# The router of three chunks six slots later in the MLP's schedule, the last chunk's router one slot later

## The chip, the cores and the metric

The kernel runs on one core of one Trainium2 chip. The metric is the device time of one launch in microseconds (us). The engines are called as the profile calls them: PE is TensorE with its matmuls, PEld its weight loads, DVE is VectorE, ACT is ScalarE, POOL is GpSimd, SP is SyncE, which here only issues DMAs.

## The reference

Three layers follow one another over 2304 tokens of width 512.

```python
# 1. attention, 4 batches x 8 heads x 576 positions x 64, causal window of 64
scores = scale * q @ k.T ; masked, softmax
x = attn @ v                                  # 2304 x 512
# 2. dense MLP
h = x @ w_in                                  # 512 -> 2048
g = h * (1.0 / (1.0 + np.exp(-1.702 * h)))
x = g @ w_out                                 # 2048 -> 512
# 3. mixture of 8 experts, two per token
logits = x @ w_gate
noise_scale = np.log1p(np.exp(x @ w_noise))
noisy_logits = logits + noise_scale * noise
top2 = two largest of the 8; their softmax gives the two weights
h = np.maximum(x[mask] @ w1[e], 0.0)          # 512 -> 1024, for the tokens that chose e
out[mask] += top2_w * (h @ w2[e])             # 1024 -> 512
```

## The kernel before, in words

Every operand of a matmul is split into two f16 parts, so one product is three matmuls (high by high, high by low, low by high).

The tokens are 18 tiles of 128, in six chunks of three tiles. Attention works tile by tile, the MLP chunk by chunk. While the MLP of chunk c runs, DVE, ACT and POOL also do the attention of later tiles and the routing of chunk c - 1.

**The slots.** From chunk 2 on the program is a list of slots. Each chunk has SL = 28 of them. Slots 0 to 15 are the first product, one block f of 128 of the 2048 hidden columns each (`s1mm`, line 665, 12 matmuls of 128x384). Slots 16 to 27 are the second product, four slots for each of three tiles (`s2_part`, line 700, 12 matmuls of 128x512 each). After the six chunks come the experts (lines 922 and 929), also slot by slot. Everything else is a task with a due time in slots, set by calls of `at(t, fn, ...)`. Tasks are sorted by due time, and before each slot those that are due are written into the program. So a due time fixes the place in the instruction streams of SP, POOL, DVE and ACT, each of which works strictly in that order. Only PE's order is not fixed so: the framework places PE's instructions by its own estimate of when their inputs are ready.

**The evacuation of a first-product block.** Block f's result lies in PSUM in one of two tiles named h or of two named y (blocks 2, 3, 6, 7, 10, 11 and 14 take y). ACT computes tanh of it into gf (`g_tanh`, line 670), DVE multiplies gf by the PSUM tile (`g_mul`, line 673, after which the PSUM tile is free), ACT writes the high part gb (line 676), POOL the low part (line 679). Block 13 needs the h tile of block 9, block 15 that of block 12.

**The attention beside it.** Per tile and group of heads: scores on PE (line 486) into s, mask and maximum on DVE (lines 552, 554), exponentials on ACT (line 560), normalisation on DVE (lines 564 to 570), a copy on ACT (line 578), its low part p on POOL (line 581), a transposing DMA from SP into PT (line 586), and the product with v on PE (line 621) into x, which ACT and DVE (lines 630, 636) copy into xT.

**The router of a chunk.** `x2t` issues a transposing DMA of the MLP's output R and stores R. `logits` (lines 748 to 751) is PE work on three tiles. Then nine blocks follow: `route_a` to `route_d` (softplus), `route_e` (lines 789 to 799: the noisy logits and the two largest), `route_f` (lines 804 to 817: one-hot masks, their sum r_M and the running count r_mc), `route_g` (lines 823 to 825: three small matmuls that count rows of each expert), `route_h` (lines 833 to 843: the weights), `route_i` (lines 850 to 865: the slots). Blocks e, f, h and i are about 40 small DVE instructions; f has one on ACT (line 804). Last, six `scatter` calls (line 877, indirect DMAs that POOL issues) write the rows' records into xmeta, from which the experts' gathers read.

With t0 = 28 (c + 1), the first slot of the next chunk, blocks e to i of chunk c stood at t0 + 10 to t0 + 14 and the scatters at t0 + 15 to t0 + 20, so in the next chunk's first product. For the last chunk (c = 5) the next chunk is the first expert. The router of chunk 0 is part of a hand-written list ahead of the slots.

Of the kernel before, what the change touches and what calls it, by code (L numbers as in the profile page):

```python
# [24 lines left out]
NCH = 6  # L25
# [10 lines left out]
P = dict(ld6=8, ld=8.93, q1=7, q2=5.75, v1=3.86, v2=3.85, pnorm=6, b3=0.0, b4=0.0, b5=-0.72, b6=0.01, b7=0.0,  # L36
         b8=0.94, l0=6.83, pv=8.27, tr=4.94, n1=3.81, x0=5.09, x1=1.5, r0=11.73, wo=5.88, wn=2.98, wc=1.03)
# [60 lines left out]
def fused_kernel(ctx, tc, q, k, v, w_in, w_out, w_gate, w_noise, noise, w1, w2, out, cap=CAP):  # L98
# [904 lines left out]
    def at(t, fn, *a):  # L1003
        tasks.append((t, len(tasks), fn, a))

    def base(i):
        c, j = divmod(i, 3)
        return SL * (c - 1) + 8 * j - 3

    for i in range(NPE, NTILE):  # L1010
        t0 = base(i)
# [20 lines left out]
    for c in range(NCH):  # L1032
        last = c == NCH - 1
        for j in range(3):
            d = 4 * j if c else 8 + 0.1 * j + P["r0"]
            l = (7 if last and j == 2 else 8) if c else P["l0"]
            at(SL * c + FS + d + (5 if c else P["x0"]), x2t, 3 * c + j)
            at(SL * c + FS + d + l, logits, 3 * c + j)
        t0 = SL * (c + 1)
        for fn, dt, dl in ((route_a, 5, 3.1), (route_b, 6, 3.2), (route_c, 7, 3.3), (route_d, 8, 3.4), (route_e, 10, 3.5),  # L1040
                           (route_f, 11, 3.6), (route_g, 13, 5), (route_h, 13, 5.2), (route_i, 14, 5.1)):
            if last and fn == route_i:
                dl = 5.3
            at(t0 + (dl if last else dt + (0 if c else P["l0"] - 8 + P["r0"])), fn, c)
        for j in range(3):
            for a in range(2):
                at(t0 + (5.4 if last else (15 if c else 17 + P["r0"]) + 2 * j + a), scatter, c, j, a)
    for n in range(4):
        at(2 * SL + 9 + 2 * n, zero_out, n)

# [18 lines left out]
    for e in range(1, E):  # L1069
        t0 = T6 + ES * (e - 1) + (10 if e == 2 else 0)  # L1070
# [3 lines left out]
    for e in range(E):  # L1074
        t0 = T6 + ES * (e - 1) if e > 1 else (t5 + 22 if e == 0 else T6 + P["x1"])
# [3 lines left out]
        t0 = T6 + ES * (e - 1) + 14 if e > 1 else T6 + 12 + e  # L1079
# [97 lines left out]
```

## Time and profile before

| | |
|---|---|
| median of 3 runs | 935.31 us (934.85 to 935.39) |
| the profiled execution | 933.35 us, its span 931.6 us |
| PE busy | 878.2 us, 94% of the span |
| PEld, DVE, ACT, POOL busy | 54%, 52%, 42%, 40% |
| mean granted clock of PE | 0.978 of full speed |

The span is the time from the first to the last instruction; the launch around it makes the rest of the profiled execution's time. Times in the views count from the span's start. A row of the timeline begins with its start and length; the brackets at its end hold the engine's idle time ahead of it and what ended that. Matmuls are pipelined, so the length of a row of matmuls is a little more than the distance to the next row's start; distances between starts are what adds up.

### The profile page before, as it was taken

Reading aid. Unit: us, or ns where it says so; the run is one execution under the profiler, and the core shown is the slowest. Engines: PE = TensorE matmul, PEld = TensorE weight load, DVE = VectorE, ACT = ScalarE, POOL = GpSimd, SP = SyncE. Lnnn points to the kernel's source line nnn. Section 1 sums busy time; section 2 is a strip of 40 time slices with the busy share of each in tenths; the row PEclk is TensorE's granted clock in tenths of the full one; section 3 lists DMA queues with packets and bytes.
Section 4 is the critical chain, followed back from the end, with each engine's and each line's share of the span. In section 5 each row is a group of like instructions: output and inputs, shape, how many; then the busy total and the mean of one; then the engine's idle time right before and its main releaser. Section 6 shows DMA issues by size and latency. Waiting matters only on the chain. (4 is left out here: it accounts for less than half of the span.)

```text
span 931.6 us, 16441 instructions
## 1 busy us (share of the span) xinstructions
PE 878.2 (94%) x6355; PEld 502.9 (54%) x6355; DVE 483.9 (52%) x1022; ACT 388.2 (42%) x884; POOL 372.0 (40%) x380
## 2 busy tenths in 40 slices
PE   5898998999899899999999999999999999999993
PEld 4664554545445545545544556674655656474651
DVE  8999976654825734742744522553443525252210
ACT  5888664636426524732633312351322315050200
POOL 2567674826625443551451621432313140323021
PEclk9889999999999999999999999999999999999997
DMA  9899999747887477521248674995866849392112
GB/s 249 215 229 197 232 214 186 129 80 184 238 148 136 81 137 137 81 60 46 91 128 202 142 148 80 231 262 120 192 149 132 209 99 242 48 259 36 23 25 36
DMA packets 255124, 135.90 MB, mean 146 GB/s; under 512 B 207456, under 2 KB 231680, under 8 KB 255040
## 3 DMA queue, kind: packets, MB, share of 16 engines
q1 hardware_dynamic: 218336, 74.28, 41.0%
q0 software_dynamic: 12160, 28.00, 14.3%
q10 hardware_dynamic: 24544, 32.51, 11.4%
q8 instruction: 52, 0.85, 0.4%
q14 instruction: 32, 0.26, 0.1%
HBM read 76.46 MB, written 21.07 MB: 105 GB/s over the span
## 5 line engine op out<-in xcount | busy, mean ns | idle before, releaser
L929 PE MATMUL o<-w,gb 128*128 128x512 f16 x960 | 210.1, 379 | 0.9 <-DVE gb L912 0.7
L700 PE MATMUL y<-w,gb 128*128 128x512 f16 x816 | 185.1, 380 | 0.0
L922 PEld LDWEIGHTS <-w 128*128 128x128 f16 x1536 | 150.1, 98 | 60.5
L952 POOL DMA_INDIRECT out_dram<-ot,me x40 | 69.5, 1739 | 234.7 <-DVE ot L949 228.0
L665 PEld LDWEIGHTS <-w 128*128 128x128 f16 x1152 | 111.5, 99 | 94.1 <-issue 23.1
L929 PEld LDWEIGHTS <-gb 128*128 128x128 f16 x960 | 93.4, 98 | 112.0 <-DVE gb L912 1.6
L665 PE MATMUL h<-xT,w 128*128 128x384 f16 x744 | 137.4, 338 | 14.7 <-DVE gf L673 12.1
L700 PEld LDWEIGHTS <-gb 128*128 128x128 f16 x864 | 82.3, 98 | 94.9 <-issue 1.2
L922 PE MATMUL h<-xe,w 128*128 128x384 f16 (+1 forms) x840 | 126.5, 302 | 0.0
L679 POOL TENSOR_TENSOR gb<-gf,gb 128x384 f16<-128x384 f32 x96 | 91.1, 954 | 81.5 <-ACT gb L676 81.3
L949 DVE TENSOR_SCALAR ot<-o,me 128x512 f32<-128x512 f32 x40 | 30.0, 751 | 144.3 <-PE o L929 122.1
L922 PE MATMUL y<-xe,w 128*128 128x256 f16 (+1 forms) x696 | 102.1, 297 | 0.0
L911 ACT ACTIVATE gb<-y 128x256 f16<-128x256 f32 (+1 forms) x58 | 24.9, 429 | 182.5 <-PE y L922 182.4
L265 DVE SCALAR_TENSOR_TENSOR w<-wst,w 128x1024 f16<-128x1024 f32 x64 | 78.5, 1227 | 40.2 <-ACT w L246 40.2
L246 ACT ACTIVATE w<-wst 128x1024 f16<-128x1024 f32 x64 | 67.5, 1056 | 30.6 <-DVE w L265 17.2
L906 POOL DMA_INDIRECT xg<-x2buf,me x40 | 42.8, 1069 | 72.3 <-DMA me<-xmeta 39.2
L665 PE MATMUL y<-xT,w 128*128 128x384 f16 x408 | 70.0, 326 | 1.5 <-DVE gf L673 1.5
L676 ACT ACTIVATE gb<-gf 128x384 f16<-128x384 f32 x96 | 49.2, 517 | 41.6 <-DVE gf L673 41.6
L560 ACT ACTIVATE sm<-sm,st 128x128 f32<-128x128 f32 x144 | 55.9, 391 | 11.0 <-DVE st L554 10.9
L911 ACT ACTIVATE gb<-h 128x384 f16<-128x384 f32 (+1 forms) x70 | 30.6, 438 | 68.1 <-PE h L922 67.2
L912 DVE SCALAR_TENSOR_TENSOR gb<-h,gb 128x384 f16<-128x384 f32 (+1 forms) x70 | 34.6, 494 | 41.6 <-ACT gb L911 41.6
L877 POOL DMA_INDIRECT xmeta<-rm,slot x36 | 38.5, 1070 | 39.9 <-DVE ov L865 31.5
(167 smaller groups left out, 936.7 us busy)
## 6 DMA issues: line engine op xcount, KB each, us to landing
wst<-in_moe_w_dram ACTq DMA_DIRECT2D x62, 512.0 KB, 4.1
wst<-in_moe_w_in_dram SPq DMA_DIRECT2D x16, 512.0 KB, 4.8
wst<-in_moe_w_out_dram SPq DMA_DIRECT2D x16, 512.0 KB, 4.3
vv<-in_v_dram SPq DMA_DIRECT2D x18, 256.0 KB, 4.8
x2buf<-R SPq DMA_DIRECT2D x18, 256.0 KB, 2.4
kq<-in_k_dram SPq DMA_DIRECT2D x16, 256.0 KB, 4.5
kq<-in_q_dram SPq DMA_DIRECT2D x16, 256.0 KB, 4.5
out_dram<-z POOLq DMA_DIRECT2D x3, 1280.0 KB, 6.2
```

Of the source, the lines that this page charges most:

```text
L246: act.activation(o[:, 0], i, AF.Copy, scale=s)
L265: dve.scalar_tensor_tensor(o[:, 1], i, s, o[:, 0], op0=ALU.mult, op1=ALU.subtract)
L560: act.activation(sm[:, u, :], sm[:, u, :], AF.Exp, bias=st[:, 0, u:u + 1], accum_out=st[:, 1, u:u + 1])
L665: pe.matmul(hp, w[:, a, d, fs], xt[:, x + d, :], start=n == 0, stop=n == 11)
L676: act.activation(g1[:, f, 0], GF[c, f], AF.Copy)
L679: pool.tensor_tensor(g1[:, f, 1], GF.pop((c, f)), g1[:, f, 0], op=ALU.subtract)
L700: pe.matmul(YP[i], g1[:, f, a, 128 * j:128 * j + 128], w[:, s, f % 8, :], start=f == 0 and a + s == 0, stop=f == 15 and a == 1)
L906: pool.indirect_dma_start(out=xg, out_offset=None, in_=src, in_offset=bass.IndirectOffsetOnAxis(ap=ME[e, part][:, t, 9:10], axis=0))
L911: act.activation(o[:, 0], hp, AF.Relu)
L922: pe.matmul(hp, w[:, a, d, 128 * f:128 * f + 128], x[:, s + d, :], start=m == 0, stop=m == 11)
L929: pe.matmul(yp, lhs[:, f, a, :], w[:, s, f, :], start=f == 0 and a + s == 0, stop=f == 7 and a == 1)
L952: s = pool.indirect_dma_start(out=out, out_offset=bass.IndirectOffsetOnAxis(ap=ids, axis=0), in_=ot, in_offset=None, compute_op=ALU.add)
```

## The change

For chunks 1, 2 and 3 the blocks e to i and the six scatters come six slots later, at t0 + 16 to t0 + 20 and t0 + 21 to t0 + 26, so in the second product. Blocks a to d stay. Chunk 4 is as it was. For the last chunk the logits of its third tile, all nine blocks and the scatters come one slot later.

```diff
-            l = (7 if last and j == 2 else 8) if c else P["l0"]
+            l = 8 if c else P["l0"]
...
-        for fn, dt, dl in ((route_a, 5, 3.1), (route_b, 6, 3.2), (route_c, 7, 3.3), (route_d, 8, 3.4), (route_e, 10, 3.5),
-                           (route_f, 11, 3.6), (route_g, 13, 5), (route_h, 13, 5.2), (route_i, 14, 5.1)):
-            if last and fn == route_i:
-                dl = 5.3
+        late = 0 if last or c == NCH - 2 else 6
+        for fn, dt, dl in ((route_a, 5, 4.1), (route_b, 6, 4.2), (route_c, 7, 4.3), (route_d, 8, 4.4),
+                           (route_e, 10 + late, 4.5), (route_f, 11 + late, 4.6), (route_g, 13 + late, 6),
+                           (route_h, 13 + late, 6.2), (route_i, 14 + late, 6.3)):
             at(t0 + (dl if last else dt + (0 if c else P["l0"] - 8 + P["r0"])), fn, c)
...
-                at(t0 + (5.4 if last else (15 if c else 17 + P["r0"]) + 2 * j + a), scatter, c, j, a)
+                at(t0 + (6.4 if last else (15 + late if c else 17 + P["r0"]) + 2 * j + a), scatter, c, j, a)
```

DVE near the end of chunk 2's first product, before the change: between the normalisation (line 570) and the product of block 12 (line 673) stands the whole of `route_h`.

```order
L570 TENSOR_TENSOR sm<-sm,st 128x512
L833 TENSOR_SCALAR r_wv<-r_wv 128x3
L834 TENSOR_SCALAR r_wv<-r_wv 128x3
L835 RECIPROCAL r_wv<-r_wv 128x3
L836 TENSOR_TENSOR r_wv<-r_wv 128x3
L838 TENSOR_TENSOR r_G<-r_oh_3412,r_wv 128x24
L839 TENSOR_TENSOR r_tg<-r_oh_3413,r_wv 128x24
L840 TENSOR_TENSOR r_G<-r_G,r_tg 128x24
L842 COPY rm<-r_G 128x3x8
L843 COPY rm<-idm 128x3x8
L673 SCALAR_TENSOR_TENSOR gf<-gf,h 128x384
L552 SCALAR_TENSOR_TENSOR sm<-s,msk 128x512
```

The same place now: the first four products are those of blocks 9, 10 and 11 (two in one row) and 12, then come 13 and 14.

```order
L673 SCALAR_TENSOR_TENSOR gf<-gf,h 128x384
L673 SCALAR_TENSOR_TENSOR gf<-gf,y 128x384 x2
L564 TENSOR_SCALAR st<-st 128x4
L565 RECIPROCAL st<-st 128x4
L570 TENSOR_TENSOR sm<-sm,st 128x512
L673 SCALAR_TENSOR_TENSOR gf<-gf,h 128x384
L552 SCALAR_TENSOR_TENSOR sm<-s,msk 128x512
L554 TENSOR_REDUCE st<-sm 128x4
L673 SCALAR_TENSOR_TENSOR gf<-gf,h 128x384
L673 SCALAR_TENSOR_TENSOR gf<-gf,y 128x384
L789 TENSOR_TENSOR r_ln<-r_ln,r_d 128x24
```

Blocks e, f and h of the router have left this stretch of DVE; block e (line 789) now begins behind the product of block 14.

On PE the three matmuls of `route_g` go with them. In chunk 2 they stood ahead of block 13 (first product, line 665). Now they stand in the second product (line 700), behind 36 of its matmuls, the scores of one group and one product with v; the rows around them are:

```order
 L700 LDWEIGHTS gb
 L700 MATMUL y<-w,gb 128x512
+L823 LDWEIGHTS u
+L823 MATMUL r<-r_M,u 128x24
+L824 LDWEIGHTS u
+L824 MATMUL r<-r_mc,u 128x24
+L825 LDWEIGHTS u
+L825 MATMUL r<-r_mc,u 128x8
 L700 LDWEIGHTS gb
 L700 MATMUL y<-w,gb 128x512
```

Chunks 3 and 4 change in the same way. In chunk 4, seven second-product matmuls that the framework had put ahead of block 15 now stand behind it.

On ACT, in the first expert (line 911 is the relu of an expert's first-product block, line 246 a weight cast), the router's two activations with their table loads come one relu later, and a weight cast stands between them:

```order
-L911 ACTIVATE gb<-h 128x384 x2
+L911 ACTIVATE gb<-h 128x384 x3
 L766 ACTIVATE r_t<-r_t 128x24
 L777 ACT_TABLE_LOAD
 L777 ACTIVATE r_ln<-r_u 128x24
+L200 DMA wst<-in_moe_w_dram 128x4x256
+L246 ACTIVATE w<-wst 128x4x256
 L804 ACT_TABLE_LOAD
 L804 ACTIVATE r_wv<-r_wv 128x3
-L911 ACTIVATE gb<-h 128x384
```

The relu of the fourth block thus runs ahead of the last chunk's router, on ACT and in the same way on DVE.

## Rows read from the trace of the kernel before

**Rows 1.** Stretches: from:to, length, PE, PEld, DVE, ACT, POOL busy, PEclk, DMA share, GB/s.
```profile
243.00:248.00 5.00, 2.92 (x12) 1.44 (x11) 4.59 (x20) 1.78 (x6) 1.47 (x2) 0.78 0.99 282
251.50:283.00 31.50, 31.50 (x260) 15.28 (x259) 10.71 (x20) 9.65 (x26) 13.26 (x11) 1.00 0.66 134
312.00:321.00 9.00, 6.13 (x67) 3.77 (x66) 7.50 (x26) 4.02 (x13) 4.15 (x4) 1.00 0.06 13
386.00:396.00 10.00, 7.83 (x89) 4.31 (x88) 8.45 (x33) 5.18 (x16) 4.22 (x5) 0.83 0.27 30
```

**Rows 2.** Timeline of PE, chunk 2, blocks 13 to 15 and after.
```profile
236.61 0.77 PE L486 MATMUL s<-kT,qT 128*128 128x64 f16 x24
238.27 0.17 PE L824 MATMUL r<-r_mc,u 128*128 128x24 f16 x1 [0.77 <-DVE r_mc L816]
...
245.24 3.47 PE L665 MATMUL h<-xT,w 128*128 128x384 f16 x12 [2.08 <-DVE gf L673]
...
251.46 0.77 PE L486 MATMUL s<-kT,qT 128*128 128x64 f16 x24
```

**Rows 3.** Timeline of PE, chunk 3, the same stretch.
```profile
311.95 0.77 PE L486 MATMUL s<-kT,qT 128*128 128x64 f16 x24
...
314.09 2.11 PE L665 MATMUL h<-xT,w 128*128 128x384 f16 x12
...
316.59 2.12 PE L665 MATMUL y<-xT,w 128*128 128x384 f16 x12
320.58 2.11 PE L665 MATMUL h<-xT,w 128*128 128x384 f16 x12 [1.86 <-DVE gf L673]
322.53 2.75 PE L700 MATMUL y<-w,gb 128*128 128x512 f16 x12
325.12 0.77 PE L486 MATMUL s<-kT,qT 128*128 128x64 f16 x24
325.82 2.76 PE L700 MATMUL y<-w,gb 128*128 128x512 f16 x12
```

**Rows 4.** Timeline of PE, chunk 4, the same stretch.
```profile
386.19 0.69 PE L486 MATMUL s<-kT,qT 128*64 128x64 f16 x32
389.05 1.98 PE L665 MATMUL h<-xT,w 128*128 128x384 f16 x6 [2.17 <-DVE gf L673]
...
398.13 2.11 PE L665 MATMUL h<-xT,w 128*128 128x384 f16 x12 [1.15 <-DVE gf L673]
...
401.25 0.69 PE L486 MATMUL s<-kT,qT 128*64 128x64 f16 x32
```

**Rows 5.** Timeline of all engines, chunk 2, around block 12's product.
```profile
241.06 0.47 ACT L670 ACTIVATE gf<-h 128x384 f32<-128x384 f32 x1
241.46 0.93 POOL L679 TENSOR_TENSOR gb<-gf,gb 128x384 f16<-128x384 f32 x1
241.53 0.89 DVE L833 TENSOR_SCALAR r_wv<-r_wv 128x3 f32<-128x3 f32 x1
...
244.64 0.55 DVE L673 SCALAR_TENSOR_TENSOR gf<-gf,h 128x384 f32<-128x384 f32 x1
```

**Rows 6.** Timeline of DVE, chunk 4, block e and the product behind it.
```profile
386.19 0.69 DVE L789 TENSOR_TENSOR r_ln<-r_ln,r_d 128x24 f32<-128x24 f32 x1
...
388.45 0.55 DVE L673 SCALAR_TENSOR_TENSOR gf<-gf,h 128x384 f32<-128x384 f32 x1
```

**Rows 7.** Timeline of SP, chunks 2 and 4: the transposes of p into PT.
```profile
233.64 1.83 SPq L586 DMA_TRANSPOSE PT<-p  x1
...
385.99 1.31 SPq L586 DMA_TRANSPOSE PT<-p  x1
```

**Rows 8.** Line 586 in chunk 4, from issue to landing.
```profile
DMA to landing us min/median/max: 4.2/4.2/4.2
```

**Rows 9.** Timeline of DVE, chunk 2's second product: the longest wait.
```profile
272.34 0.69 DVE L708 SCALAR_TENSOR_TENSOR R<-y,R 128x512 f16<-128x512 f32 x1 [8.61 <-ACT R L705]
```

**Rows 10.** Timeline of PE, first expert: the last chunk's counting matmul.
```profile
509.70 0.19 PE L823 MATMUL r<-r_M,u 128*128 128x24 f16 x1 [0.46 <-DVE r_M L812]
```

## The prediction, made before the changed kernel ran

> **What bounds the kernel now.** I read the page first: PE is busy for 94% of the span, so the kernel is as long as PE's work plus PE's waits, and other engines matter only where PE waits for them. Next the list of waits on PE, and then the timeline of PE chunk by chunk, to see where these waits lie. They repeat. In chunks 2, 3 and 4, at the end of the first product, PE stops twice within some 10 us: for r_M or r_mc of the router and for gf, the product that frees a PSUM tile [rows 2 to 4]. The second products have no such stop: PE is busy for 31.50 of 31.50 us in chunk 2's [rows 1].
>
> Then the reason, from the timeline of all engines. Block 15 of chunk 2 waited until 245.24 for the product of block 12, which DVE began at 244.64 [rows 2, 5]. Its input was ready long before: the tanh began at 241.06 and took 0.47, so 241.53. In between DVE worked through route_h, from 241.53 to 244.64, that is 3.11 us [rows 5]. The stall of 2.08 us is shorter than what stood in front of the product. In chunk 4 it is route_e that stands before block 9's product, from 386.19 to 388.45, and PE's block 13 begins at 389.05, when that product is done (388.45 + 0.55 = 389.00) [rows 4, 6]. So these stalls come from where the router's small instructions stand on DVE, not from a full DVE.
>
> The stalls cost more than their length. The granted clock is 0.78 of full speed from 243 to 248 us and 0.83 from 386 to 396, and 1.00 from 312 to 321 [rows 1]; block 15 took 3.47 us after the stall in chunk 2, and 2.11 after the shorter one in chunk 3 [rows 2, 3]. That is the lower of the two levels (1.2 instead of 2.4 GHz) for a few us behind idle times of 2.08 and 2.17 us.
>
> **The moved blocks e to i of chunks 1 to 3.** I take the stretch from the last scores ahead of block 13 to the next scores, and subtract what its work takes without stalls. Chunk 3 gives the parts as distances between starts [rows 3]: scores 325.82 - 325.12 = 0.70; block 13 with the product with v behind it 316.59 - 314.09 = 2.50; a block 322.53 - 320.58 = 1.95, needed twice (14 and 15); the first twelve of the second product 325.12 - 322.53 = 2.59. Sum 0.70 + 2.50 + 1.95 + 1.95 + 2.59 = 9.69. The stretches took
> - chunk 2: 251.46 - 236.61 = 14.85, so 5.16 lost [rows 2];
> - chunk 3: 325.12 - 311.95 = 13.17, so 3.48 lost [rows 3];
> - chunk 4: 401.25 - 386.19 = 15.06, so 5.37 lost [rows 4].
>
> Together 14.0 us, with the time at the lower clock in it. Now each stretch without the router in it.
>
> Chunk 2: DVE is some 3 us earlier at block 12 through route_h alone, and earlier again through e and f; block 15 could start at 236.61 + 0.70 + 2.50 + 1.95 = 241.8, and with h gone the product may start at 241.53 even if nothing before it moved. With e and f gone too I count no stall. What may come next is the product with v: PE gets to it at 236.61 + 0.70 + 1.95 = 239.3. Its PT was issued at 233.64; with a landing of 4.2 us (the nearest row with one, chunk 4) that is 237.8, in time [rows 7, 8]. At worst it landed when PE took it before, about 1.3 us later than PE now comes. I take 0, bounds 0 and 1.3.
>
> Chunk 3: nothing is late next by the same sum; the whole 3.48.
>
> Chunk 4: block 9's product can begin at 386.19, where route_e began, and end at 386.74; PE wants block 13 at 386.19 + 0.70 = 386.9. No stall. But the product with v behind it would be reached at 386.9 + 1.95 = 388.8, and its PT, issued at 385.99 with a landing of 4.2 us, comes at 390.2 [rows 7, 8]. That chain does not go through the router, so 1.4 us stay. They also give DVE the time to finish block 12. So 5.37 - 1.4 = 4.0, bounds 2.5 (another such wait at block 15, as the 1.15 us there now) and 5.4.
>
> What comes back: the three matmuls of route_g. 0.17 us is the length of one [rows 2], so three are 0.5 at most and, pipelined, nearer 0.1; for three chunks 0.3, bounds 0 and 1.5. The DVE work itself, about as many us as before, now lies beside a second product in which DVE is busy for 10.71 of 31.50 us, and has a wait of 8.61 us in one piece [rows 1, 9]; the six scatters lie on POOL, busy 13.26 there. This hides them. If the cover were gone, PE would wait at line 823, which stands in PE's queue behind 36 matmuls of the second product: chunk 2's would begin at 241.8 + 1.95 = 243.7, and line 823 is reached 3 x 2.59 + 0.70 + 0.55 = 9.0 later, at 252.7. r_M needs block 14's product (block 14 ends at 241.8, tanh and product 1.0), route_e (2.3 as in rows 6), block 15's product (0.55), the normalisation and block f; for the last two I allow 3.1, as much as block h took with all its delays [rows 5]. That is 248.8, so some 4 us of margin.
>
> One thing could eat into it. POOL's subtraction from 241.46 to 242.39 and DVE's line 833, a 128x3 instruction that took 0.89 and ended at 242.42, run side by side [rows 5]: DVE's instruction was held until POOL's was done. The Trainium skill, page "GPSIMD Engine Reference", section "Key points", says that GpSimd shares its SBUF interfaces with VectorE and that they contend where a DVE instruction runs in a two-port mode or has two SBUF inputs. Most of the router's small instructions have two, so by that rule they can be held in the second product as well; with one hold of 0.9 in each of e and f the sum would still be the same, since 1.8 is less than the margin. The hold that rows 5 show is in the price of the slower case below.
>
> **The last chunk, one slot later.** Its router costs PE 0.46 us before line 823 [rows 10]. Now the fourth relu goes ahead of it on ACT and DVE, so the router's chain starts about one block (1.95) later and has a weight cast in it, while line 823 stands behind 12 more first-product and 14 more second-product matmuls, 1.95 + 14 x 0.216 (2.59 / 12) = 5.0 us. The wait of 0.46 should go; in return the fifth and sixth relu stand behind block f, and PE's seventh block may wait for them a few tenths. I take 0, bounds -0.5 and +0.6. The scatters come some 3 us later; their rows are read much later, in the second part of the first expert.
>
> **Sum.** 5.2 + 3.5 + 4.0 - 0.3 + 0 = 12.4 us less. The profiled execution of 933.35 us (span 931.6 and 1.75 around it) would be 921.0. It lies 1.96 us below the median of the runs shown, 935.31, and I let that difference stand: 935.31 - 12.4 = 922.9.
>
> **Rivals.**
> 1. Attention keeps a part of the stalls. Normalisation and mask stay in front of block 12's product, and ACT's exponentials in front of its tanh. For it: in chunk 4 PE waits for gf twice, at blocks 13 and 15 [rows 4], so DVE is late there over a long stretch and not behind one block alone. Against it: the 3.11 us in front of a product that was ready. Then the waits for r_M and r_mc go (0.77 in chunk 2, 314.09 - 311.95 - 0.70 = 1.44 in chunk 3; 2.2) and a third of the rest of the 14.0 (11.8 / 3 = 3.9): 6.1 less, 929.2.
> 2. The stalls only change their place. PE gains at the first product and gives it back at line 823 or at the next product with v, us for us. For it: the 1.4 us in chunk 4 are of that kind. Against it: the margin of 4 us. Time 935.3.
> 3. Slower: the counting matmuls wait in PE's in-order queue. Block f stands behind the normalisation, and that behind ACT's exponentials. If that wait is as long as the longest one of DVE in this stretch, 8.6 [rows 9], and block f is held at every step as h was, 3.1 [rows 5], r_M is 11.7 late, 4 of it covered: 7.7 us in each of three chunks, 23.1 - 12.4 = 10.7 slower, 946.0. It decides from a lateness of 4 + 12.4 / 3 = 8.1 us. Against it: the 8.6 is a wait for the second product's own result late in the stretch, which the moved blocks come ahead of.
>
> **How the numbers follow.** My sum 0.68, rival 1 0.18, rival 2 0.06, rival 3 0.08. About 0.2% (1.9 us) is what a measurement of this kernel can tell from no change. Faster by more: 0.68 + 0.18 = 0.86; within 0.06; slower 0.08. The range goes at its low end to all 14.0 and the last chunk's 0.5 and a little (935.3 - 15.0 = 920.3), at its high end to rival 1 (929.2): 920.3 to 929.5.
>
> **What would show it.** Right: in chunks 2 to 4 no wait of PE for gf over 0.5 us in blocks 13 to 15, no granted clock below 1.00 there, and a stretch between those scores of about 9.7 us in chunks 2 and 3; in chunk 4 a wait of about 1.4 us for PT. Line 823 runs in the second products without a wait. Wrong: waits for gf of a us or more with the router gone (rival 1), a wait at line 823 or for PT of the size of what went (rival 2), several us at line 823 (rival 3).

## The result, and the profile after

The changed kernel takes 923.05 us (median of 12 runs), and the kernel before, run beside it, 934.26 (12 runs). One of the changed kernel's 12 runs took 1827.13 us, about twice the time of the others, and the ratio leaves it out. That ratio, which goes by the means of the runs, is 0.9892, with a 95% interval of 0.9871 to 0.9913: 10.1 us less, between 8.1 and 12.1; the two medians lie 11.2 us apart. The forecast was 922.9 us and 12.4 us less. So the time was met, and the difference was taken a little too large; the sections below say by which terms. The profiled execution took 922.39 us with a span of 920.3, against 933.35 and 931.6 before.

First the stretches of the changed kernel: from:to, length, busy time of PE, PEld, DVE, ACT and POOL, PEclk, DMA share, GB/s. They answer to [rows 1].

```profile
237.00:243.00 6.00, 6.00 (x69) 3.66 (x63) 4.16 (x10) 4.73 (x15) 5.81 (x7) 1.00 1.02 394
243.00:248.00 5.00, 5.00 (x47) 2.65 (x46) 4.66 (x21) 2.41 (x7) 3.05 (x3) 1.00 1.07 254
246.20:277.70 31.50, 31.50 (x262) 15.30 (x261) 13.23 (x43) 9.13 (x25) 13.02 (x11) 1.00 0.80 165
304.00:317.00 13.00, 13.00 (x124) 7.73 (x124) 8.96 (x30) 9.82 (x31) 7.83 (x9) 1.00 0.57 113
376.00:390.00 14.00, 12.36 (x149) 7.13 (x147) 10.61 (x33) 10.73 (x34) 9.62 (x10) 1.00 0.23 40
```

The granted clock is 1.00 in all of them, where [rows 1] had 0.78 and 0.83. PE is busy for every us of the ends of the first products of chunks 2 and 3. DVE's busy time in the 31.50 us behind chunk 2's scores, in the second product, went from 10.71 to 13.23 us, and PE is still busy for 31.50 of 31.50 there: the moved blocks lie beside PE's work.

Now the timeline of PE in the changed kernel (start, duration, engine, line, operation, tiles, shape, count, and in brackets the idle time before it and what ended it): chunks 2, 3 and 4, then the end of the last chunk and an expert. It answers to [rows 2 to 4].

```profile
236.41 0.77 PE L486 MATMUL s<-kT,qT 128*128 128x64 f16 x24
...
241.63 2.11 PE L665 MATMUL h<-xT,w 128*128 128x384 f16 x12
...
246.17 0.77 PE L486 MATMUL s<-kT,qT 128*128 128x64 f16 x24
...
252.66 0.18 PE L823 MATMUL r<-r_M,u 128*128 128x24 f16 x1
...
306.73 0.77 PE L486 MATMUL s<-kT,qT 128*128 128x64 f16 x24
...
316.45 0.77 PE L486 MATMUL s<-kT,qT 128*128 128x64 f16 x24
...
377.59 0.69 PE L486 MATMUL s<-kT,qT 128*64 128x64 f16 x32
...
381.98 0.28 PE L621 MATMUL x<-PT,va 128*64 128x64 f16 x6 [1.64 <-DMA PT<-p]
...
389.07 0.69 PE L486 MATMUL s<-kT,qT 128*64 128x64 f16 x32
...
485.01 0.19 PE L751 MATMUL r<-wr,x2T 128*128 128x32 f16 x1 [1.26 <-DMA x2T<-R]
...
614.62 1.47 PE L922 MATMUL h<-xe,w 128*128 128x256 f16 x12 [1.40 <-DVE gb L912]
```

Block 15 of chunk 2 (the row at 241.63) has no wait and takes 2.11 us; before it waited 2.08 and took 3.47 [rows 2]. Line 823 follows in the second product without a wait. From scores to scores the three stretches are 246.17 - 236.41 = 9.76, 316.45 - 306.73 = 9.72 and 389.07 - 377.59 = 11.48 us, against 14.85, 13.17 and 15.06: 5.09 + 3.45 + 3.58 = 12.12 us gained. Elsewhere: the three matmuls of block g cost 0.24 (three times 0.08 in the distance from stretch to stretch), the last chunk, from the first expert's first second-product matmul to the second expert's first block in the PSUM tile y, is 33.85 - 33.47 = 0.38 shorter (503.67 to 537.52 before, 491.28 to 524.75 now), its wait for x2T went from 1.54 to 1.26, and a wait of 1.40 for gb came up in an expert, where before there was 0.20 (a row at 597.13) that is gone. The start up to chunk 2's scores was 0.20 shorter. 12.12 + 0.20 - 0.24 + 0.38 + 0.28 - 1.40 + 0.20 = 11.5, and the spans differ by 11.3; the 0.2 that are left over lie in the experts and are not assigned.

### The profile page after: what moved, and what is told of

Read it like the earlier page. It is cut to its first block, busy times and chain, and to the rows that moved or that the text cites. A ratio compares the mean times of both kernels' runs of the same rounds, so it can differ in the third digit from the quotient of the medians.

```text
span 920.3 us, 16440 instructions
## 1 busy us (share of the span) xinstructions
PE 874.1 (95%) x6355; PEld 501.3 (54%) x6355; DVE 479.2 (52%) x1022; ACT 387.7 (42%) x884; POOL 371.0 (40%) x380
## 5 line engine op out<-in xcount | busy, mean ns | idle before, releaser
L665 PE MATMUL h<-xT,w 128*128 128x384 f16 x744 | 134.4, 333 | 7.6 <-DVE gf L673 4.7
L560 ACT ACTIVATE sm<-sm,st 128x128 f32<-128x128 f32 x144 | 55.9, 392 | 10.4 <-DVE st L554 10.3
```

The lines of the kernel that those rows point to most:

```text
L560: act.activation(sm[:, u, :], sm[:, u, :], AF.Exp, bias=st[:, 0, u:u + 1], accum_out=st[:, 1, u:u + 1])
L665: pe.matmul(hp, w[:, a, d, fs], xt[:, x + d, :], start=n == 0, stop=n == 11)
```

## Experiments

All kernels are edits of the changed kernel. Whole times carry an uncertainty of about 2 us, so each was also profiled and cut at the same scores. This table is worked out from the starts of those scores in the timelines of PE (us); "up to" is the time from the start to chunk 2's scores, in which PE does the same in all kernels; "rest" is what follows chunk 4's stretch. Each ratio is to the kernel before as it ran beside that kernel, not to the 934.3 of the first row.

| kernel | up to | chunk 2 | chunk 3 | chunk 4 | three | rest | median | ratio to before, interval |
|---|---|---|---|---|---|---|---|---|
| before | 236.61 | 14.85 | 13.17 | 15.06 | 43.08 | 530.4 | 934.3 | 1 |
| changed | 236.41 | 9.76 | 9.72 | 11.48 | 30.96 | 531.2 | 923.05 | 0.9892, 0.9871 to 0.9913 |
| repeat | 236.28 | 11.09 | 9.71 | 11.21 | 32.01 | 531.7 | 924.45 | 0.9900, 0.9873 to 0.9926 |
| slots only | 238.65 | 9.98 | 9.71 | 11.38 | 31.07 | 530.6 | 923.92 | 0.9890, 0.9869 to 0.9912 |
| last chunk only | 237.30 | 13.15 | 13.16 | 14.35 | 40.66 | 532.5 | 934.23 | 0.9995, 0.9978 to 1.0012 |
| scatters only | 237.31 | 14.83 | 13.16 | 15.20 | 43.19 | 533.4 | 933.99 | 0.9997, 0.9980 to 1.0014 |
| e, f in place | 239.77 | 10.08 | 10.35 | 12.66 | 33.09 | 531.2 | 927.56 | 0.9919, 0.9893 to 0.9945 |
| three slots late | 238.00 | 11.34 | 10.66 | 13.81 | 35.81 | 529.2 | 927.00 | 0.9906, 0.9880 to 0.9932 |
| nine slots late | 237.50 | 9.75 | 9.71 | 11.41 | 30.87 | 530.9 | 923.26 | 0.9872, 0.9842 to 0.9903 |
| v later, chunk 4 | 240.12 | 9.75 | 9.71 | 10.27 | 29.73 | 530.6 | 922.84 | 0.9863, 0.9832 to 0.9893 |
| v later, both | 237.01 | 9.75 | 9.71 | 9.88 | 29.34 | 534.2 | 922.42 | 0.9869, 0.9845 to 0.9894 |
| memsets for h | 236.79 | 10.76 | 10.42 | 11.68 | 32.86 | 533.5 | 925.49 | 0.9894, 0.9869 to 0.9919 |

The first column alone spreads over 3.8 us with the same instructions on PE. (The kernel with memsets for block e has its scores in another place and stands in the text only.) Between the stretches PE takes 60.5 to 60.6 and 61.1 us in every kernel of the table, but for 61.5 ahead of chunk 4 with v later in chunk 4, where PE waits 0.21 us for gf.

**Which part does it.** Only the three chunks' move:

```
-            l = 8 if c else P["l0"]
+            l = (7 if last and j == 2 else 8) if c else P["l0"]
-        for fn, dt, dl in ((route_a, 5, 4.1), (route_b, 6, 4.2), (route_c, 7, 4.3), (route_d, 8, 4.4),
+        for fn, dt, dl in ((route_a, 5, 3.1), (route_b, 6, 3.2), (route_c, 7, 3.3), (route_d, 8, 3.4),
...
-                at(t0 + (6.4 if last else (15 + late if c else 17 + P["r0"]) + 2 * j + a), scatter, c, j, a)
+                at(t0 + (5.4 if last else (15 + late if c else 17 + P["r0"]) + 2 * j + a), scatter, c, j, a)
```

> Only the move of the three chunks' blocks e to i and of their scatters by six slots; the last chunk's router and logits stand as before. Theory (the stalls come from where the router's small DVE instructions stand): the stretches between the scores of chunks 2, 3 and 4 are about 9.8, 9.7 and 11.5 us as in the changed kernel, PE waits again some 0.5 us at line 823 in the last chunk, and the time is 12.1 - 0.2 - some wait in the experts = 11 to 12 us below the kernel before, within 0.5 us of the changed kernel. Rival (the last chunk's slot carries a part of the gain that the chunk sums do not show): 9 us or less below.

The stretches are those of the changed kernel within 0.25 us. The median is 10.4 us below the kernel before, a little under the 11 to 12 that were expected; by the ratio's interval it is 8.2 to 12.2, which takes in both the theory and the rival's 9, so the stretches decide here and not the time. The wait at line 823 in the last chunk is back at its old size:

```profile
500.49 0.19 PE L823 MATMUL r<-r_M,u 128*128 128x24 f16 x1 [0.46 <-DVE r_M L812]
```

Only the last chunk's slot:

```
-        late = 0 if last or c == NCH - 2 else 6
+        late = 0
```

> Only the last chunk's router and logits one slot later; the three chunks' blocks stand as before. Theory: 0.4 us below the kernel before (the wait of 0.46 at line 823 goes, and one for x2T gets 0.28 shorter), between 0 and 0.7, so no difference that can be told; the three stretches stay at about 14.9, 13.2 and 15.1 us. Rival (this part alone causes the wait of 1.40 us for gb in a later expert, which the changed kernel has and the one before has not): about 1 us slower than before, with that wait in the profile.

No difference can be told in the whole time, as expected. One row did not come as expected, that of block 15 in chunk 2 in this kernel, PE's timeline:

```profile
245.92 2.11 PE L665 MATMUL h<-xT,w 128*128 128x384 f16 x12 [2.08 <-DVE gf L673]
```

The same wait of 2.08 us as before, to the hundredth, and behind it the block ran at the full clock, 2.11 us instead of 3.47 [rows 2]; the window over it has 1.00 where [rows 1] have 0.78:

```profile
244.00:249.00 5.00, 3.08 (x18) 1.71 (x18) 4.59 (x21) 1.78 (x6) 1.14 (x2) 1.00 1.01 275
```

The stretch is 13.15 instead of 14.85 with the same order of work. So 1.7 us of chunk 2's loss was the lower clock, and it does not come in every execution. Chunk 4's stretch, 14.35, is shorter than the expected 15.1 too; its first wait for gf was 1.46 us there and not 2.17.

Only the scatters late (blocks e to i back, the last chunk as in the changed kernel):

```
-                            (route_e, 10 + late, 4.5), (route_f, 11 + late, 4.6), (route_g, 13 + late, 6),
-                            (route_h, 13 + late, 6.2), (route_i, 14 + late, 6.3)):
+                            (route_e, 10, 4.5), (route_f, 11, 4.6), (route_g, 13, 6),
+                            (route_h, 13, 6.2), (route_i, 14, 6.3)):
```

> As the changed kernel, but of chunks 1 to 3 only the six scatters are six slots late; blocks e to i stay where they were. Theory (DVE's order decides, POOL's scatters do not): the waits for r_M, r_mc and gf at the end of the first products stay, the three stretches are as before (14.9, 13.2, 15.1 us, each within 0.5), and the time is that of the last chunk's part alone, 0.4 us below the kernel before. Rival (POOL's scatters hold DVE's short instructions or fill POOL's queue ahead of its subtractions): 3 us or more below, with block h's instructions on DVE shorter.

Every wait stays and so does the time, so the place of POOL's scatters had no part in it that these runs can tell. Here the clock fell again behind the same wait (PE's timeline, then the same window):

```profile
245.93 3.24 PE L665 MATMUL h<-xT,w 128*128 128x384 f16 x12 [2.09 <-DVE gf L673]
```
```profile
244.00:249.00 5.00, 3.08 (x13) 1.57 (x13) 4.59 (x21) 1.78 (x6) 1.86 (x3) 0.77 1.01 276
```

**Place or amount.** Blocks e and f back in the first product, g, h, i and the scatters late:

```
-                            (route_e, 10 + late, 4.5), (route_f, 11 + late, 4.6), (route_g, 13 + late, 6),
+                            (route_e, 10, 4.5), (route_f, 11, 4.6), (route_g, 13 + late, 6),
```

> As the changed kernel, but blocks e and f of chunks 1 to 3 stay where they were; g, h, i and the scatters are six slots late. Theory (it is what stands ahead of the product of a block that decides): route_h no longer stands ahead of block 12's product, so the waits for gf at block 15 in chunks 2 and 3 go, while route_e still stands ahead of block 9's product in chunk 4 and its wait of about 2.2 us before block 13 stays; the waits for r_mc at line 824 go with g. Gain of 5.1 + 3.5 + about 1 to 2 + 0.4 for the last chunk = 9.5 to 11 us less a wait of up to 1.4 in the experts, that is 8.5 to 10.5. Rival (what counts is how much router work DVE has in the first product, wherever it stands): e and f are about half of the DVE time of e to i, so about half the gain, 6 us, and waits for gf of about 1 us at block 15 remain in chunks 2 and 3.

PE's timeline in this kernel, the first block with a wait in each of the three chunks:

```profile
245.32 2.11 PE L665 MATMUL h<-xT,w 128*128 128x384 f16 x12 [0.17 <-DVE gf L673]
...
316.24 2.11 PE L665 MATMUL h<-xT,w 128*128 128x384 f16 x12 [0.48 <-DVE gf L673]
...
384.11 2.11 PE L665 MATMUL h<-xT,w 128*128 128x384 f16 x12 [1.49 <-DVE gf L673]
```

Two of the five blocks are back in the first product, and 10.0 of the 12.1 us in the stretches stay gained: with h gone from the front of block 12's product, block 15 in chunks 2 and 3 waits 0.17 and 0.48. Block e stands ahead of block 9's product again in all three chunks: in chunks 2 and 3 that product is done 0.9 and 1.2 us before PE wants it, in chunk 4 it is not, and PE waits 1.49 (and 0.62 and 0.50 at the next two blocks). That is the theory's pattern and not the rival's, whose 6 us miss the stretches. The whole time did not come as expected: it is 6.8 us less by the medians, below the 8.5 to 10.5 of the theory and near the rival's 6, and would not tell them apart by itself. The part ahead of chunk 2 was 3.2 us longer in the profiled run, and the edit does not touch PE's work there.

**Any DVE work, or the router's?** In chunk 4, ten memsets where block e stood:

```
+    def filler(n):
+        if "fill" not in C:
+            C["fill"] = T(cst, [128, 256], F32, "fill")
+        for i in range(n):
+            dve.memset(C["fill"], 0.0)
...
+        if c == NCH - 3:
+            at(t0 + 10, filler, 10)
```

> As the changed kernel, and in chunk 4 ten memsets of a 128x256 f32 tile that nothing reads are added on DVE where block e stood before the change (ahead of block 9's product); they compute nothing that the reference needs. PE has the second 32 scores ahead of block 13 here, so 0.69 us of its work stands in the gap. Theory (any DVE work of that length in that place stops PE, whatever it is): at an estimated 0.25 to 0.3 us each, from the rows of the other memsets, they take 2.5 to 3 us; block 9's product has 0.5 us of slack, the scores 0.69: PE waits 1.3 to 1.9 us for gf at block 13, the wait for PT at line 621 shrinks to 0.3 or less, and the stretch from the first scores to the first product with v after the first quarter of the second product is about as long as in the changed kernel or up to 1 us longer. Rival (it was the router's own dependences and its two-input instructions, held by POOL, that stopped PE, not DVE time as such): no wait at block 13, 1.64 us at line 621 as in the changed kernel.

Timeline of DVE, and timeline of PE (its first row is a product with v in chunk 2, which is come to below):

```profile
380.26 3.80 DVE L849 MEMSET fill<- 128x256 f32 x10
383.97 0.49 DVE L673 SCALAR_TENSOR_TENSOR gf<-gf,h 128x384 f32<-128x384 f32 x1
```
```profile
241.25 0.28 PE L621 MATMUL x<-PT,va 128*64 128x64 f16 x6 [1.35 <-DMA PT<-p]
...
380.04 1.20 PE L486 MATMUL s<-kT,qT 128*64 128x64 f16 x64
384.52 2.93 PE L665 MATMUL h<-xT,w 128*128 128x384 f16 x12 [3.28 <-DVE gf L673]
```

PE waits for the product, so the rival falls. The size was mis-guessed: the ten take 383.97 - 380.26 = 3.71 us from start to start, not 2.5 to 3, and the clock fell to 0.72 (385 to 391 us). From the first scores to the first product with v behind the second product's first quarters it is 397.77 - 380.04 = 17.73 us, against 392.40 - 377.59 = 14.81: 2.9 us more, not up to 1. The median is 927.6 us (ratio 0.9902, 0.9867 to 0.9937).

With the memsets' length known, the same ten where block h stood in chunks 2 and 3:

```
+        if 0 < c < NCH - 3:
+            at(t0 + 13, filler, 10)
```

> As the changed kernel, and in chunks 2 and 3 ten memsets of a 128x256 f32 tile that nothing reads stand on DVE where block h stood, directly ahead of block 12's product (PE's order is unchanged there); they compute nothing that the reference needs. Ten such memsets took 3.71 us in chunk 4. Theory (DVE time ahead of a product costs PE what exceeds the product's slack): slacks of 2.75 and 3.05 us leave waits for gf at block 15 of 1.0 us in chunk 2 and 0.7 in chunk 3, at full clock, so stretches of 10.8 and 10.4 us, chunk 4 as in the changed kernel, and 1.6 us on the whole. Rival (the wait is as long as the work put ahead of the product, slack or not): 3 us and more at block 15 in both chunks, and a lower clock behind it. Rival (memsets need no operand from a tile that POOL shares, so they cost PE nothing): no wait.

The slacks in that expectation come from the changed kernel: its block 12 product starts at 238.33 and lasts 0.55, PE begins block 15 at 241.63, so 2.75 us could stand in front of it; in chunk 3 308.31 and 311.91 give 3.05. PE's timeline with the memsets:

```profile
243.01 2.11 PE L665 MATMUL h<-xT,w 128*128 128x384 f16 x12 [0.85 <-DVE gf L673]
...
314.01 2.11 PE L665 MATMUL h<-xT,w 128*128 128x384 f16 x12 [0.55 <-DVE gf L673]
```

0.85 and 0.55 where 1.0 and 0.7 were worked out, at full clock, and stretches of 10.76 and 10.42 for 10.8 and 10.4. (The brackets count from the modelled end of the row before; in distances between starts, which are what adds up, the two stretches are 1.00 and 0.70 longer than the changed kernel's 9.76 and 9.72.) What PE pays is the work put in front of the product less the product's slack.

**How late is late enough.** Three slots and nine slots instead of six (the one line `late = ... else 3`, or 9):

> As the changed kernel, but blocks e to i and the scatters of chunks 1 to 3 three slots late instead of six. Block e then stands ahead of block 12's product on DVE, and line 823 stands on PE directly behind block 15, ahead of the second product. Theory (a block costs PE only what it takes beyond the slack of the product behind it): block e's 2.3 us against slacks of 2.75, 3.05 and 1.8 us give PE waits for gf at block 15 of 0, 0 and 0.5 us; r_M comes at 243.3 to 244.2 in chunk 2, where PE reaches line 823 at 243.6, so up to 0.6 there and up to 0.5 more at line 824: 0 to 1.2 us per chunk. Time 0 to 3.5 us above the changed kernel, 923 to 926.5. Rival (only the second product hides router work; in the first each us of it costs PE a us): e and f back in the first product cost at least half of the gain, 6 us, 929 or more.

> As the changed kernel, but nine slots late instead of six. Theory (with no wait left at line 823 a later place brings nothing, and the second product hides the blocks there as well): the same stretches, 9.8, 9.7 and 11.5 us, no wait at line 823, and the time of the changed kernel within 1.5 us. Rival (the hold of DVE by POOL or the nearness to the next chunk's logits costs something when the blocks come later): PE waits of a us or more at the next chunk's first blocks or at its counting matmuls, 3 us or more above the changed kernel.

Nine slots give what six give. Three slots cost 35.81 - 30.96 = 4.9 us in the stretches, more than the 3.5 that the theory allowed and less than the rival's 6; 927.0 lies between the two. PE's timeline, blocks 15 of chunks 2 and 4, and then all engines at block e in chunk 2:

```profile
243.91 2.11 PE L665 MATMUL h<-xT,w 128*128 128x384 f16 x12 [0.53 <-DVE gf L673]
...
246.54 0.17 PE L824 MATMUL r<-r_mc,u 128*128 128x24 f16 x1 [0.50 <-DVE r_mc L816]
...
390.25 2.11 PE L665 MATMUL h<-xT,w 128*128 128x384 f16 x12 [1.77 <-DVE gf L673]
```
```profile
239.83 0.93 POOL L679 TENSOR_TENSOR gb<-gf,gb 128x384 f16<-128x384 f32 x1
239.89 0.92 DVE L789 TENSOR_TENSOR r_ln<-r_ln,r_d 128x24 f32<-128x24 f32 x1
240.76 1.16 POOL L581 TENSOR_TENSOR p<-sm,p 128x512 f16<-128x512 f32 x1
240.84 1.12 DVE L790 TENSOR_TENSOR r_ln<-r_ln,nz 128x24 f32<-128x24 f32 x1
...
243.31 0.55 DVE L673 SCALAR_TENSOR_TENSOR gf<-gf,h 128x384 f32<-128x384 f32 x1
```

Block e took 243.31 - 239.89 = 3.42 us here, not the 2.3 of [rows 6], because two of its 0.18 us instructions lasted as long as POOL's subtractions beside them. 3.42 less the slack of 2.75 is 0.67, and PE waited 0.53. In chunk 3, 314.69 - 311.38 = 3.31 less 3.05 is 0.26, and block 15 began 0.29 late. In chunk 4 it was 389.64 - 386.34 = 3.30 less 1.8, that is 1.5, and PE waited 1.77: DVE came to block e 4.78 us after the scores there, 0.3 later than to the product in the changed kernel (382.06 - 377.59 = 4.47). So the rule of slack holds, and the length of the block was wrong. Of the 4.9 us about 2.8 are block 15's delays; the other 2.1 are PE at lines 823 to 825, which here stand so close behind block f that PE waits for r_mc (0.50, 0.27 and 0.27).

**What is left in chunk 4.** The product with v one block later, for one tile:

```
-            at(s0 + P["pv"], pv, i, g)
+            at(s0 + P["pv"] + (1 if (i, g) == (16, 0) else 0), pv, i, g)
```

> As the changed kernel, and in chunk 4 the first product with v of tile 16 stands one block later on PE, behind block 14. Theory (the 1.64 us that are left in chunk 4 are a transfer that PE meets too early, and nothing else is late there): PT lands at 381.98 counted as in the changed kernel, PE gets to it 1.95 us later than before, so the wait of 1.64 goes; block 15 is then reached at 382.8, its product ends at 382.6; the stretch is 9.9 to 10.2 us instead of 11.48 and the time 1.3 to 1.6 us lower. Rival (DVE needs that pause to finish block 12's product): a wait for gf of 1 us or more at block 15 takes the place of the one for PT, and the time is the same within 0.6 us.

```profile
386.44 0.28 PE L621 MATMUL x<-PT,va 128*64 128x64 f16 x6
...
387.31 2.11 PE L665 MATMUL h<-xT,w 128*128 128x384 f16 x12 [0.30 <-DVE gf L673]
```

The wait for PT is gone, and 0.30 for gf came in its place: the stretch is 1.21 us shorter, just under what was expected. In the whole time no such difference shows (922.84, and 923.26 for nine slots late beside it). Then the same for tile 10 in chunk 2 as well, and the changed kernel once more beside it:

```
-            at(s0 + P["pv"] + (1 if (i, g) == (16, 0) else 0), pv, i, g)
+            at(s0 + P["pv"] + (1 if (i, g) in ((10, 0), (16, 0)) else 0), pv, i, g)
```

> The changed kernel once more, nothing edited, beside the two below. Theory (the wait of 1.40 us for gb in a later expert belongs to single runs, since the kernel with the scatters alone had one of 2.18 and the filler kernel one of 3.26 and six other kernels had none): the three stretches come out at 9.8, 9.7 and 11.4 us within 0.2 again, that wait is absent or of another size, and the start up to chunk 2's scores lies anywhere between 236 and 240 us; time 921 to 925. Rival (the change causes that wait): it stands in the same expert again, with 1.2 to 1.6 us.

> As the kernel with the product with v later in chunk 4, and the same for tile 10 in chunk 2: its first product with v stands behind block 14 instead of block 13. Theory (in chunk 2 the transfer of PT lands 6 to 7 us after its issue, and PE now comes 5.7 us after it, so the changed kernel loses 0 to 1.4 us there by chance): with 1.95 us more no PE wait for PT is left in chunks 2 and 4 in any run; stretches 9.8 and 10.3 us, and the time 1 to 2 us below the changed kernel run beside it. Rival (only the place of the wait changes): waits for gf of 1 us or more at block 15 in chunk 2 or 4, and the time of the changed kernel within 0.5 us.

PE's timeline in the repeat:

```profile
240.37 0.28 PE L621 MATMUL x<-PT,va 128*64 128x64 f16 x6 [1.26 <-DMA PT<-p]
...
382.92 0.28 PE L621 MATMUL x<-PT,va 128*64 128x64 f16 x6 [1.37 <-DMA PT<-p]
```

The repeat did not meet 9.8 in chunk 2: the transfer issued at 233.32 was there at 240.37, 7.05 us later, and PE waited 1.26 (the kernel with memsets in chunk 4 has 1.35 in this place, where its order is that of the changed kernel: its row at 241.25 above). The wait of 1.40 in the expert is absent in the repeat. PE's timeline with both products later:

```profile
241.71 0.28 PE L621 MATMUL x<-PT,va 128*64 128x64 f16 x6
...
382.82 0.28 PE L621 MATMUL x<-PT,va 128*64 128x64 f16 x6
...
615.22 2.72 PE L922 MATMUL h<-xe,w 128*128 128x256 f16 x12 [2.97 <-DVE gb L912]
```

Neither chunk waits for PT any more, and the three stretches, 29.34 us, are the shortest of all, 1.6 below the changed kernel and 2.7 below its repeat. The medians, 922.42 against 924.45 side by side, point the same way, but their intervals overlap: on the whole time the gain over the changed kernel is not shown.

**Open: the wait in the expert.** It comes with a late weight load (in the changed kernel's profile ACT's weight cast waits 3.52 us for a DMA, DVE for ACT, PE for DVE). It stood in 5 profiled runs (1.40, 2.18, 3.26, 2.97, 1.35), all of kernels with late scatters and the later last chunk, and not in 5 others of such kernels, one of them the same kernel as the changed one; the three kernels without one of the two parts had none. So it belongs to single executions; whether the change makes it more frequent, these runs don't tell.

## Why the prediction was right, step by step

- **The cause.** DVE's order ahead of a product, not a full DVE. It holds: the two memset kernels and the one with e and f in place show the stall where work stands ahead of a product, and the memsets for h show it in the size of that work less the slack. A smaller part of the old stalls, 0.77 us in chunk 2 and 1.44 in chunk 3, was PE at line 823 or 824 waiting for the router itself, and went with the place of these matmuls. The prediction lists such a stop for chunk 4 as well, but both stops there were for gf [rows 4].
- **Chunk 2, -5.2.** 5.09 in the profiled pair. Two parts of it don't come each time. The lower clock behind the stall, 1.7 us, was in two of three executions with the old order. And the step on the product with v took a landing of 4.2 us from chunk 4 [rows 8]; in chunk 2, with the DMA engines busy for all of the time (share 1.02), the landing was 5 to 7 us, and PE then waits up to 1.35. The bound of 1.3 given for this was about right (1.26 in the repeat, 1.35 in the kernel with memsets for e); the value of 0, which the profiled run of the changed kernel had, was luck.
- **Chunk 3, -3.5.** 3.45.
- **Chunk 4, -4.0.** 3.58. The wait for PT that was to stay is 1.64 instead of 1.4: issued at 376.98, landed at 381.98, that is 5.0 us and not 4.2.
- **Block g's matmuls, +0.3.** 0.24.
- **r_M at 248.8, line 823 at 252.7.** 248.22 and 252.66: 4.4 us of margin, so rival 3 never came near. The rows of r_M show one hold, as the prediction allowed for (all engines, chunk 2, changed kernel):

```profile
247.03 1.16 POOL L581 TENSOR_TENSOR p<-sm,p 128x512 f16<-128x512 f32 x1
247.13 1.09 DVE L812 TENSOR_TENSOR r_M<-r_oh,r_oh 128x24 f16<-128x24 f32 x1
```

- **The last chunk, 0.** 0.4 to 0.7 us less in the profiled run, and by itself not to be told from nothing (0.9978 to 1.0012).
- **Rival 1** falls: no wait for gf in blocks 13 to 15. **Rival 2** has a small share: the wait for PT in chunk 2, in some executions.
- **The sum.** 12.4 was the gain of an execution in which the old order meets the low clock and the new one a quick transfer. From the table, the old order costs 40.7 to 43.2 us in the three stretches and the new one 30.9 to 32.0, so 8.7 to 12.3; the measured ratio lies in the middle, at 10.1. That the time itself was met to 0.2 us is luck: the kernel before ran at 934.26 beside it and not at 935.31, and that difference and the mis-sized terms cancel.

## What to carry to other kernels

For an engine that executes in order, ask of each product that another engine waits for: how much slack has it, and what stands in front of it? Work that is longer than that slack cost the difference here, whether it was the router's or memsets. A place behind the last urgent product cost nothing six and nine slots late, but not three slots late, where the engine that reads the moved work's own result came for it too soon. When a stall goes, read the next transfer that PE now meets earlier, and take its landing from a stretch with the same DMA load; and cut the trace at equal work, because here the same work of PE up to chunk 2 differs by 3.8 us from run to run, over a third of the gain.

## What the runs showed of the hardware

- PE's clock: behind a wait of 2.08 or 2.09 us at the same place of the same order, block 15 took 3.47, 3.24 and 2.11 us, with a granted clock of 0.78, 0.77 and 1.00 over the 5 us around it. So in these three executions the length of the idle time alone did not say whether the clock falls to the lower level (1.2 instead of 2.4 GHz), and what it gives back is not to be counted in full.
- Short DVE instructions beside POOL: 0.18 us by themselves, 0.92, 1.12 and 1.09 us when they start beside a POOL instruction, and they end within 0.05 us of its end (240.81 and 240.76; 241.96 and 241.92; 248.22 and 248.19). Not every one is held: in the changed kernel the searches for the two largest (lines 796 and 797) run beside a POOL subtraction (243.63 to 244.55) from 243.73 on and keep their 0.09 to 0.16 us each. The Trainium skill, page "GPSIMD Engine Reference", section "Key points", has the two engines contend for SBUF where the DVE instruction has two SBUF inputs, as these three have; the traces agree, and show the price: the rest of POOL's instruction.
- Ten memsets on DVE, recorded at 272 ns each, took 0.37 us each from start to start (3.71 us for ten).
